# Units 12 to 23 of a chunked RWKV-5 attention beside a SwiGLU block: 64 steps of two batches a unit instead of 128 steps of one

## The chip, the cores and the metric

The kernel runs on one core of a Trainium2 chip. The core has a matrix engine (PE, with its weight loads shown apart as PEld), a vector engine (DVE), a scalar engine (ACT), GpSimd (POOL) and SyncE (SP), which here issues most of the DMAs. The metric is device microseconds of one execution, lower is better.

## The reference, cut to what matters

```python
# r, k, v: (4 batches, 8 heads, 768 steps, 48); w, u: (8, 48)
for t in range(S):
    cur = einsum('bhd,bhe->bhde', u[None] * kt, vt)
    y[:, :, t] = einsum('bhd,bhde->bhe', rt, state + cur)
    state = w[None, :, :, None] * state + einsum('bhd,bhe->bhde', kt, vt)
x = y.transpose(0, 2, 1, 3).reshape(B * S, H * D)          # (3072, 384)
g = x @ w_gate                                             # w_gate, w_val: (384, 1536)
out = (g / (1 + exp(-g)) * (x @ w_val)) @ w_out            # w_out: (1536, 384)
```

All of it is in float32.

## The kernel before, in words

**Units.** The 768 steps of each of the 4 batches are cut in 6 chunks of 128 steps. A unit i is chunk i // 4 of batch i % 4, so there are 24 units. In a unit the scores of a head are a 128x128 product of turned keys and turned r, masked below the diagonal. On the diagonal stands the sum of r, k and u (`own_sum`, DVE; `diagonal`, ACT: eight times the identity scaled by a column of `du`). The decay w is worked into k and r beforehand by tables (`scale_k`, `scale_r`, POOL), so that the state needs one factor a chunk.

**What a unit does on PE.** `scores(i)` (L459) writes two banks of PSUM, one for the even and one for the odd heads. `outputs(i)` (L512) makes the turned y, 384 rows by 128 steps, in 32-row tiles, four of them side by side in the array: for each tile one product of the state `Z` with turned r, and one or two of `v_ld` with the masked scores `At`. ACT copies the bank to `xT` (L516). `update(i)` (L527) makes the chunk's part of the new state, which DVE adds to `Z` (L539) and POOL multiplies by w to the 128th (L540). Units 20 to 23 need no update.

**From unit 12 on** the scores are computed in halves of 64 keys: 64x128 and 64x64 pieces, so that the quarter above the diagonal is not computed. So that the DMAs that turn k and r can stay inside such halves, the steps of the upper four heads stand swapped in the partitions (`places`, `in_order`, the second mask). k and r are not turned on PE from unit 10 on: `move_blocks` has SP move 32x32 blocks of `hats` within SBUF (L416, 16 DMAs a unit from unit 12 on), and `turn_blocks` has DVE transpose them in place (L437, twice a unit).

**Order.** Each engine's order is that of the recorded program. Step s of the loop (L1288) prepares unit s + 1 (`scale_k`, `scale_r`, `own_product` on POOL), computes `scores(s - 1)`, and from step 12 on `outputs(s - 2)` and `update(s - 2)` right behind it. The rest of PE's time is filled with the feed-forward work of finished units, which stands in `todo`: `gaps(s, n)` takes a share of it at five places in a step. This work is `gate_value` (L550), `project` (L625) and, from pair 2 on, `three_step` (L806), a product of 3x3 blocks in 15 rounds instead of 18. Its sums are evicted from four banks by DVE and ACT (L830), its gates are computed by ACT (L837), and its weight sums are made by POOL (L736). Each `feed` also takes one waiting diagonal (`small`) and one waiting masked copy (`lazy`). The attention's own banks are a ring of four (`next_psum`): a step takes two for scores, one for outputs, one for the update.

**SP's queue** holds, in order, the loads of k and r for unit s + 3 (6 DMAs), the moves for unit s + 1 (16) and the loads of v for unit s + 1 (6). On even steps the loads of k and r stand behind those of v, since `scale_r` comes late there.

Step 26 ends the loop's work; from there a tail of `three_units` and `project_thirds` runs to the end.

Of the kernel before, what the change touches and what calls it, by code (L numbers as in the profile page):

```python
# [15 lines left out]
P = 128  # L16
# [6 lines left out]
def fast(  # L23
# [47 lines left out]
    w128 = cst.tile([P, HP], FP32, name="w128")  # L71
    held = cst.tile([P, HP], FP32, name="held")
# [27 lines left out]
    Z = [cst.tile([P, HP, D2], FP32, name=f"Z{b}") for b in range(B)]  # L100
# [23 lines left out]
    SWAPPED = 12  # L124

    def places(i, n):

        if i < SWAPPED:
            return [(slice(0, P), slice(0, n), 0)]
        return [  # L130
            (slice(0, P), slice(0, n // 2), 0),
            (slice(0, 64), slice(n // 2, n), 64),
            (slice(64, P), slice(n // 2, n), -64),
        ]

    def load(i):
        c, b = divmod(i, B)
        for src, dst in zip((k, r), raw(i)):
            for p, h, o in places(i, H):
                rows = slice(P * c + p.start + o, P * c + p.stop + o)  # L140
                sp.dma_start(out=dst[p, h], in_=src[b, h, rows, :].rearrange("h t d -> t h d"))

    def load_v(i):
        c, b = divmod(i, B)
        for e in range(2):
            for p, a, o in places(i, HP):
                rows = slice(P * c + p.start + o, P * c + p.stop + o)
                sp.dma_start(
                    out=v_ld[i % 4][p, a, 64 * e : 64 * e + D],
                    in_=v[b, :, rows, :].rearrange("(a e) t d -> e t a d", e=2)[e][:, a],  # L150
                )
# [129 lines left out]
    for z in Z:  # L281
        pool.memset(z[:], 0.0)
# [14 lines left out]
    def warm(n, bank=None):  # L297
# [12 lines left out]
    pool.memset(mask[:], 1.0)  # L310
    pool.affine_select(
        out=mask[:], in_=mask[:], compare_op=ALU.is_gt, fill=0.0,
        base=0, pattern=[[0, 2], [1, P]], channel_multiplier=-1,
    )
    pool.memset(mask[0:64, 1, 64:P], 0.0)
    pool.memset(mask[64:P, 1, 0:64], 1.0)
# [24 lines left out]
    def at(i, a):  # L341

        return HP - 1 - a if i >= BLOCKS and i % 2 == (i < SWAPPED) else a

# [19 lines left out]
    def diagonal(i, on_act=None):  # L364

        du = dus.pop(i)
        on_act = on_act or (HP if i < 4 else H)
# [28 lines left out]
    def move_blocks(i):  # L396
# [4 lines left out]
        if i < SWAPPED:  # L401
# [10 lines left out]
        for m in range(4):  # L412
            for q in range(4):
                src = h[32 * q : 32 * q + 32, P * first + 32 * m : P * first + 32 * m + 1]
                dst = h[32 * m : 32 * m + 32, P * 31 + 32 * q : P * 31 + 32 * q + 1]
                sp.dma_start(  # L416
                    out=bass.AP(
                        tensor=dst.tensor, offset=dst.offset,
                        ap=[list(dst.ap[0]), [-P, 2 * HP], [1, 32]],
                    ),  # L420
                    in_=bass.AP(
                        tensor=src.tensor, offset=src.offset,
                        ap=[list(src.ap[0]), [P * step, 2 * HP], [1, 32]],
                    ),
                )

    def turn_blocks(i):
# [5 lines left out]
        for n, (dst, src) in enumerate(((kT[i % 2], blocks[0]), (turned[i], blocks[1]))):  # L433
            if i < SWAPPED:
# [8 lines left out]
    def scores(i):  # L443
# [4 lines left out]
        whole, left, right = slice(0, P), slice(0, 64), slice(64, P)  # L448
        if i < SWAPPED:
            parts = [(a, whole, whole) for a in range(HP)]  # L450
        else:
            parts = []
            for a in range(HP // 2):
                parts += [(a, left, whole), (a, right, right)]
                parts += [(a + HP // 2, right, whole), (a + HP // 2, left, left)]
        for a, keys, cols in parts:
            for e in range(2):
                rows = slice(64 * e, 64 * e + D)
                pe.matmul(  # L459
                    ps[e][keys, a, cols],  # L460
                    kT[i % 2][rows, at(i, a), keys], turned[i][rows, at(i, a), cols],
# [3 lines left out]
        def masked_copy(e):  # L465
            if i < SWAPPED:
                dst = At[i % 2][:].rearrange("p (a e) t -> p a e t", e=2)[:, :, e]
                m = mask[:, 0].bitcast(INT32).unsqueeze(1).to_broadcast([P, HP, P])
                dve.copy_predicated(dst, m, ps[e][:])
                return  # L470
            dst = At[i % 2][:].rearrange("p (o a e) t -> p o a e t", o=2, e=2)[:, :, :, e]
            m = mask[:].bitcast(INT32).unsqueeze(2).to_broadcast([P, 2, HP // 2, P])
            dve.copy_predicated(dst, m, ps[e][:].rearrange("p (o a) t -> p o a t", o=2))
# [6 lines left out]

    def outputs(i):

        c, b = divmod(i, B)
# [5 lines left out]
        def in_order(x, a):  # L491
            if i < SWAPPED or a < HP // 2:
                return x
            return bass.AP(
                tensor=x.tensor, offset=x.offset + 64,
                ap=[list(x.ap[0]), [-64, 2], [1, 64]],
            )

# [19 lines left out]
    def update(i):  # L518
        c, b = divmod(i, B)
        if c == NCH - 1:  # L520
            return
# [766 lines left out]
    for s in range(4, N + 2):  # L1288
        if 4 < s < N:
            own_sum(s)  # L1290
# [496 lines left out]
```

## Time and profile before

| what | us |
|---|---|
| median of 3 runs (590.78 to 591.75) | 591.72 |
| profiled execution, span from first to last instruction | 590.1 |
| median less that span | 1.6 |
| PE busy / PEld busy | 579.1 / 520.6 |
| DVE busy / POOL busy / ACT busy | 424.3 / 352.5 / 226.9 |
| scores of unit 12, the first that the change touches, start at | 156.9 |
| outputs of unit 23, the last, end at | 427.5 |
| granted PE clock, mean | 0.998 of full |

The span was taken in one profiled execution, which is not one of the three that were timed. What lies outside it, 1.6 us by the median, is the start and the end that show no instruction. A step that the change touches is therefore worth in the median what it is worth in the span. [...] Durations of PE records overlap, since matmuls are pipelined, so the time that a group takes is read from where the next group starts.

### The profile page before, as it was taken

To read this page: it belongs to the slowest core of one execution; us is meant where nothing else is said; L and a number is where in the kernel's file an instruction comes from. 1 tells how busy PE (TensorE), PEld (TensorE's weight loads), DVE (VectorE), ACT (ScalarE), POOL (GpSimd) and SP (SyncE) were. 2 spreads that over 40 slices of the span, in tenths; PEclk is the share of its full clock that TensorE was granted. 3 is DMA by queue.
4 is the path that set the end of the run, shared out by engine and by line. 5 is a ranking of instruction groups with operands and counts; after the bars stand their busy time and mean duration, and the time that the engine had idled before them with its cause. 6 is when DMAs were issued, how large, how long until landed. Compare 5 with 4: busy or idle time off the path is not lost.

```text
span 590.1 us, 13203 instructions
## 1 busy us (share of the span) xinstructions
PE 579.1 (98%) x5210; PEld 520.6 (88%) x5210; DVE 424.3 (72%) x713; ACT 226.9 (38%) x523; POOL 352.5 (60%) x375
## 2 busy tenths in 40 slices
PE   8889999999999999999999999999999999999996
PEld 7778888899888899988899988889988899988896
DVE  7878786489588877578887477879257878377682
ACT  4559786321443422244331344423134320233310
POOL 6689888989999402977600996513678970011610
PEclk9999999999999999999999999999999999999999
DMA  7999978641342323233234233200100000100001
GB/s 196 220 240 248 270 249 87 70 70 40 78 77 38 54 48 70 48 63 54 39 57 79 67 55 55 47 14 2 54 2 1 1 1 1 55 0 1 1 1 57
DMA packets 148004, 41.48 MB, mean 70 GB/s; under 512 B 138465, under 2 KB 141794, under 8 KB 147938
## 3 DMA queue, kind: packets, MB, share of 16 engines
q1 hardware_dynamic: 144770, 36.27, 30.7%
q10 hardware_dynamic: 3168, 4.33, 2.0%
q8 instruction: 42, 0.69, 0.5%
q14 instruction: 24, 0.20, 0.1%
HBM read 28.31 MB, written 4.72 MB: 56 GB/s over the span
## 4 chain that ended last, share of the span: by engine, by line
PE 95%; DVE 2%; DMA 1%; issue 0%; POOL 0%; ACT 0%; POOLq 0%; DVEq 0%
PE bank L806 32%; PE bank L625 18%; PE ring L806 13%; PE bank L550 11%; PE bank L1032 8%; PE ring L512 6%; PE ring L459 3%; PE ring L390 1%; PE ring L1032 1%; PE ring L527 1%; DMA hats<-in_r_dram 1%; PE ring L301 1%; DVE hv L830 0%; PE bank L354 0%; PE ring L305 0%
## 5 line engine op out<-in xcount | busy, mean ns | idle before, releaser
L830 DVE TENSOR_TENSOR hv<-hv,bank 128x512 f32<-128x512 f32 x132 | 87.2, 681 | 25.9 <-PE bank L806 14.0
L369 ACT ACTIVATE At<-ident,du 128x128 f32<-128x128 f32 x180 | 61.0, 398 | 14.1 <-DVE du L270 6.1
L550 PE MATMUL bank<-xT,wgv 128*128 128x256 f32 x288 | 66.2, 384 | 0.0
L806 PE MATMUL bank<-xf,wgv 128*128 128x256 f32 x256 | 65.9, 382 | 0.0
L830 ACT COPY hv<-bank 128x512 f32<-128x512 f32 x72 | 40.2, 586 | 57.1 <-PE bank L806 50.7
L550 PEld LDWEIGHTS bank<-xT,wgv 128*128 128x128 f32 x288 | 53.4, 190 | 8.0
L736 POOL TENSOR_TENSOR s<-wgv 128x256 f32<-128x256 f32 x39 | 29.8, 788 | 49.0 <-PE bank L625 48.9
L806 PEld LDWEIGHTS bank<-xf,wgv 128*128 128x128 f32 x256 | 47.8, 190 | 7.0 <-DVE kT L1077 0.6
L1086 POOL TENSOR_TENSOR hv<-At,hats 128x512 f32<-128x512 f32 x8 | 10.2, 1273 | 66.0 <-ACT At L1085 66.0
L540 POOL TENSOR_TENSOR Z<-Z,w 48x192 f32<-48x192 f32 x32 | 16.9, 528 | 36.7 <-DVE Z L539 35.5
L837 ACT ACTIVATE hv<-hv 128x512 f32<-128x512 f32 (+1 forms) x33 | 21.2, 667 | 45.4 <-DVE hv L830 45.2
L512 PE MATMUL ring<-At,v_ld 128*32 128x128 f32 x768 | 35.1, 273 | 2.1 <-ACT xT L516 1.4
L806 PE MATMUL bank<-xT,wgv 128*128 128x256 f32 x144 | 35.8, 381 | 0.0
L806 PE MATMUL bank<-xT,s 128*128 128x256 f32 x152 | 35.5, 381 | 0.0
L625 PE MATMUL bank<-wt,hs 128*128 128x192 f32 x192 | 33.7, 328 | 0.6 <-DVE hs L599 0.6
L625 PE MATMUL bank<-wo,hs 128*128 128x192 f32 x192 | 33.9, 327 | 0.0
L625 PE MATMUL bank<-wo,hv 128*128 128x192 f32 x192 | 33.4, 327 | 0.0
L512 PEld LDWEIGHTS ring<-At,v_ld 128*32 128x32 f32 x768 | 30.5, 110 | 3.3 <-ACT xT L516 1.6
L806 PEld LDWEIGHTS bank<-xT,s 128*128 128x128 f32 x152 | 28.5, 190 | 4.8 <-issue 0.8
L625 PEld LDWEIGHTS bank<-wt,hs 128*128 128x128 f32 x192 | 31.3, 190 | 1.4 <-ACT At L369 0.8
L625 PEld LDWEIGHTS bank<-wo,hv 128*128 128x128 f32 x192 | 31.6, 190 | 0.4
L625 PEld LDWEIGHTS bank<-wo,hs 128*128 128x128 f32 x192 | 31.6, 190 | 0.3
(227 smaller groups left out, 1398.9 us busy)
## 6 DMA issues: line engine op xcount, KB each, us to landing
hats<-hats SPq DMA_DIRECT2D x192, 32.0 KB, 2.0
w_bits<-in_moe_w_gate_dram SPq DMA_DIRECT2D x6, 768.0 KB, 6.1
w_bits<-in_moe_w_val_dram SPq DMA_DIRECT2D x6, 768.0 KB, 6.9
w_bits<-in_moe_w_out_dram SPq DMA_DIRECT2D x6, 768.0 KB, 6.9
out_dram<-hv ACTq DMA_DIRECT2D x22, 192.0 KB, 1.9
v_ld<-in_v_dram SPq DMA_DIRECT2D x24, 96.0 KB, 5.8
k_ld<-in_k_dram SPq DMA_DIRECT2D x8, 192.0 KB, 3.5
r_ld<-in_r_dram SPq DMA_DIRECT2D x8, 192.0 KB, 4.0
```

The source lines that it names most:

```text
L369: lambda h=h: act.activation(At[i % 2][:, h, :], ident[:], AF.Identity, scale=du[:, h : h + 1])
L459: pe.matmul(ps[e][keys, a, cols], kT[i % 2][rows, at(i, a), keys], turned[i][rows, at(i, a), cols], start=True, stop=True, skip_group_chec ...
L512: pe.matmul(ps[32 * q : 32 * q + 32, cc, :], *x, start=start, stop=stop, skip_group_check=True,)
L540: pool.tensor_mul(ze, ze, w)
L550: pe.matmul(gv[:, o, :].rearrange("p (i t) -> p i t", i=2), wt[:, c, P * f : P * (f + 1)], xT[:, 2 * g % NX : 2 * g % NX + 2, c, :], start ...
L625: pe.matmul(ps, lhs[:, f, :], rhs[:, f, :], start=(f == 0 and n in (0, 1, 4)), stop=(f == FH - 1), skip_group_check=True,)
L736: op(made[o], made[a], made[b])
L806: pe.matmul(ps[:, o], u[:, o], v, start=first and o == 0, stop=True, skip_group_check=True,)
L830: do(out, *(pair_of(wide[a][:]) if isinstance(a, str) else a for a in args))
L837: todo.append((at, lambda: act.activation(gate, gate, AF.Silu)))
L1032: pe.matmul(ps, (h[what][q] if h[what] is D_ else h[what][:, q])[:, f, :], wide["o"][what][:, f, :], start=first and f == 0 and (split or ...
L1086: todo.append((muls, lambda: on.tensor_mul(h, sg, value)))
```

## The change

From unit 12 on a unit is 64 steps of two batches: partitions 0 to 63 hold one batch, 64 to 127 the other (`part`, `pieces_of`). There are still 24 units. The units 12 to 23 are now 6 chunks of 64 steps for each pair of batches, so the state of a batch is needed again after two units, not after four.

- **Outputs.** For batch p one tile of `At` (`both(i)[:, p]`) holds the masked 64x64 scores on one half of the partitions and turned r on the other half. `v_ld` of the batch holds v on the first half and the state on the other. One product over all partitions then gives both parts of y. A unit's outputs are 32 matmuls of 64 columns; before they were 28 of 128 columns.
- **Scores** are 16 matmuls of 64 keys by 64 columns in four 64x64 tiles of the array; before, 8 had 128 columns and 8 had 64.
- **Update** is 16 matmuls of 64x48 (before 32x48) into two banks of the ring (before one), for units 12 to 21 (before 12 to 19). DVE adds in four pieces instead of two, POOL multiplies two tiles of 48x384 instead of two of 48x192, by w to the 64th (`w64`). The state stays in `v_ld`; units 8 to 11 put theirs there by two DMAs each.
- **Diagonal**: eight scaled 64x64 identities a unit go to `own`, which lies over the old `Z`. `fill(i)` is new: four DMAs of SP, two for turned r and two for `own`, into `At`, where the masked copies then write the scores (four of 64x256, before two of 128x512).
- **Order.** `outputs(s - 2)` stands ahead of `scores(s - 1)` from step 14 on, `update(s - 2)` behind it. `diagonal(s)` is taken at the start of step s and flushed before `fill(s)` at the step's end. `load_v(s)` follows `update(s - 2)`.
- **DMAs of SP for a unit**: 4 loads of k and r (6), 4 of v (6), 8 moves (16), 4 fills (none). Results of units 12 to 23 are stored in two DMAs of 64 rows instead of one of 128.
- The helpers of the swapped order go, and the tables' lower halves are copied over the upper ones once.

PE's order in step 14: `rT` and `kT` are turned r and k, `Z` is the state before, `ring` are the attention's banks, `bank` those of the feed-forward work; rows that repeat are left out. Before:

```order
L459 MATMUL ring3_98<-rT_1881,kT1_115 64x128
L459 MATMUL ring0_95<-rT_1881,kT1_115 64x128
L459 MATMUL ring3_98<-rT_1881,kT1_115 64x64
L459 MATMUL ring0_95<-rT_1881,kT1_115 64x64
L512 MATMUL ring1_96<-rT_1657,Z0_99 32x128 x4
L512 MATMUL ring1_96<-At0_112,v_ld0_107 32x128 [waits DMAHW1_49]
L527 MATMUL ring2_97<-v_ld0_107,hats_111 32x48 x16
L806 MATMUL bank2_93<-xT_88,wgv_86 128x256 [waits DVE_49]
```

Now, at the same place (L550 is the new outputs, L516 the new scores, L567 the new update, L922 the old L806):

```order
L550 MATMUL ring3_99<-At0_110,v_ld0_105 32x64 [waits DMAHW6_49,DMAHW7_49,DMAHW2_49,DMAHW0_49]
L550 MATMUL ring3_99<-At0_110,v_ld0_105 32x64
L550 MATMUL ring3_99<-At0_110,v_ld1_106 32x64 [waits DMAHW4_49,DMAHW1_49,DMAHW0_49]
L516 MATMUL ring0_96<-rT_1873,kT1_113 64x64 x2
L516 MATMUL ring1_97<-rT_1873,kT1_113 64x64 x2
L567 MATMUL ring2_98<-v_ld0_105,hats_109 64x48 x2
L567 MATMUL ring3_99<-v_ld1_106,hats_109 64x48 [waits Activation_49]
L922 MATMUL bank2_94<-xT_89,wgv_87 128x256 [waits DVE_49]
```

The outputs moved ahead of the scores, and the second bank of the update is ring3, the bank that the outputs of the same step have just filled: the update waits for ACT's copy of it.

SP's order for the steps 16 and 17, from the moves for unit 17 on (`zs` holds `own`). Before:

```order
L416 DMA hats<-hats 32x8x32 x16
L148 DMA v_ld_108<-in_v_dram 128x2x48
L148 DMA v_ld_108<-in_v_dram 64x2x48 x2
L148 DMA v_ld_108<-in_v_dram 128x2x48
L141 DMA k_ld_106<-in_k_dram 128x4x48
L141 DMA k_ld_106<-in_k_dram 64x4x48 x2
```

Now:

```order
L435 DMA hats<-hats 32x16x32 x8
L147 DMA k_ld_104<-in_k_dram 64x8x48 x2
L147 DMA r_ld_102<-in_r_dram 64x8x48 x2
L503 DMA At_110<-rT 64x512
L504 DMA At_110<-zs 64x512
L153 DMA v_ld_107<-in_v_dram 64x4x48 x2
L153 DMA v_ld_108<-in_v_dram 64x4x48 x2
```

The loads of v no longer follow the moves; the four fills (two rows of each kind) stand at the end of a step's DMAs, behind the eight moves for the next unit.

The core of the diff:

```diff
+    zs = cst.tile([P, B, HP * D2], FP32, name="zs")
+    own = zs[:].rearrange("p b x -> p (b x)")[:, 0 : 2 * H * 64].rearrange(
...
+    def part(i, p):
+        c, q = divmod(i - PAIRED, 2)
+        return 2 * q + p, PAIRED // B * P + 64 * c
...
-        for m in range(4):
-            for q in range(4):
-                src = h[32 * q : 32 * q + 32, P * first + 32 * m : P * first + 32 * m + 1]
...
+        for p in range(2):
+            for n in range(2):
+                for m in range(2):
+                    q, o = 64 * p + 32 * n, 64 * first + 32 * m
+                    src = h[q : q + 32, o : o + 1]
...
+    def fill(i):
+        rT = turned[i][:].rearrange("p a (e t) -> p (a e) t", e=2)
+        for p in range(2):
+            there, here = slice(64 - 64 * p, P - 64 * p), slice(64 * p, 64 * p + 64)
+            sp.dma_start(out=both(i)[there, p], in_=rT[there])
+            sp.dma_start(out=both(i)[here, p], in_=own[here, i % 2])
+
+    def paired_scores(i, ps):
...
+        for n in range(HP):
+            for p in range(2):
+                rows = slice(64 - 64 * p, 64 - 64 * p + D)
+                for g in range(2):
+                    o = 64 * (p ^ g)
+                    pe.matmul(
+                        ps[p][o : o + 64, n, :], kt[rows, n + HP * g, :], rT[rows, n + HP * g, :],
...
+        def masked_copy(p, g):
+            rows, o = slice(64 * p, 64 * p + 64), 64 * (p ^ g)
+            m = mask64[rows].bitcast(INT32).unsqueeze(1).to_broadcast([64, HP, 64])
+            dve.copy_predicated(both(i)[rows, p, HP * g : HP * g + HP], m, ps[p][o : o + 64])
...
+        lazy.popleft()()
+        lazy.popleft()()
+
+    def paired_outputs(i):
+        ps = next_psum(CC, P)
...
+                vz, x = v_ld[part(i, p)[0]], both(i)[rows, p]
...
+                pe.matmul(
+                    ps[32 * q : 32 * q + 32, cc, 64 * p : 64 * p + 64], *x,
...
+        act.copy(xT[:, i % NX, :, :], ps[:])
+
+    def paired_update(i):
+        if i + 2 >= N:
+            return
+        ps = [next_psum(HP, D) for _ in range(2)]
...
+                    pe.matmul(
+                        ps[p][o : o + 64, n, :], khat[i % 4][rows, h, :],
+                        v_ld[part(i, p)[0]][rows, a, 64 * e : 64 * e + D],
...
+            ze = state(slice(0, HP))
+            pool.tensor_mul(ze, ze, w64[o : o + D].unsqueeze(3).to_broadcast([D, HP, 2, D]))
...
     for s in range(4, N + 2):
+        if PAIRED <= s < N:
+            diagonal(s)
...
         gaps(s, 0)
+        if s > N:
+            outputs(s - 2)
         if 4 <= s - 1 < N:
-            while small:
-                small.popleft()()
+            if s <= PAIRED:
+                flush()
+            if s - 2 >= PAIRED:
+                outputs(s - 2)
             scores(s - 1)
+            if LATE <= s < PAIRED + 2:
+                outputs(s - 2)
             if s >= LATE:
-                outputs(s - 2)
                 update(s - 2)
+            if PAIRED <= s < N:
+                load_v(s)
             gaps(s, 1)
...
-        if s < N:
+        if s < PAIRED:
             diagonal(s)
+        elif s < N:
+            flush()
+            fill(s)
```

More of the change, by code (lines that the diff above doesn't have):

```diff
@@ L366, in diagonal @@
         du = dus.pop(i)
+        if i >= PAIRED:
+            small.extend(
+                lambda h=h: act.activation(
+                    own[:, i % 2, slot(i, h), :], ident64, AF.Identity, scale=du[:, h : h + 1]
+                )
+                for h in range(H)
+            )
+            return
         on_act = on_act or (HP if i < 4 else H)
```

233 lines of the change are left out of this document (143 added, 90 removed).

## The prediction

> **What bounds the kernel now.** I read the page first: its busy times and the chain that ended last.
>
> ```profile
> span 590.1 us, 13203 instructions
> PE 579.1 (98%) x5210; PEld 520.6 (88%) x5210; DVE 424.3 (72%) x713; ACT 226.9 (38%) x523; POOL 352.5 (60%) x375
> PE 95%; DVE 2%; DMA 1%; issue 0%; POOL 0%; ACT 0%; POOLq 0%; DVEq 0%
> ```
>
> PE is the bound: busy for 98% of the span and 95% of the chain. The next question is whether PE waits for anything in the stretch of the change. The windows answer for two steps (after the stretch: its length, the busy time of PE, PEld, DVE, ACT and POOL, the granted clock, the DMA share, GB/s), and the waits from 150 to 430 us for all of them (total, times, longest).
>
> ```profile
> 160.00:180.00 20.00, 20.00 (x199) 17.31 (x199) 16.59 (x27) 7.71 (x19) 19.14 (x26) 1.00 0.39 65
> 180.00:200.00 20.00, 20.00 (x93) 16.92 (x92) 17.19 (x25) 9.31 (x19) 18.67 (x22) 1.00 0.27 42
> ```
>
> ```profile
> PEld bank L806 <- ACT hv L830: 1.9, 6, 0.4
> PEld bank L625 <- ACT At L369: 0.8, 1, 0.8
> PE bank L625 <- DVE hs L599: 0.6, 1, 0.6
> ```
>
> PE has no gap at a clock of 1.00, and the three largest sums of its waits for other engines are 3.3 us in eight places, none above 0.8. So every PE nanosecond removed here is worth its full length, if nothing new holds PE up. But DVE is busy 83 and 86% of these windows: it has 2.8 to 3.4 us to spare in 20. Last I read PE's timeline of step 14 and the durations of L527's records.
>
> ```profile
> 175.64 0.90 PE L459 MATMUL ring<-rT,kT 48*64 48x128 f32 x32
> 176.47 0.43 PE L512 MATMUL ring<-rT,Z 112*32 112x128 f32 x8
> ...
> 177.81 0.40 PE L512 MATMUL ring<-At,v_ld 128*32 128x128 f32 x8
> 178.03 0.52 PE L527 MATMUL ring<-v_ld,hats 128*32 128x48 f32 x32
> 178.48 1.99 PE L806 MATMUL bank<-xT,wgv 128*128 128x256 f32 x8
> L527 PE MATMUL ring<-v_ld,hats x640: 204/206/231, 27.1 to 348.1; 128*32 128x48 f32 x160
> ```
>
> One step's attention takes PE 2.84 us: scores 0.83, outputs 1.56, update 0.45. These 34 us in 12 steps are all that the change can shorten.
>
> **The change part by part.** *The price of a column.* Each product stands as two records, and four tiles run side by side. The update's 32 records take 0.52 us less the 0.206 of the last one: 31 intervals of 10.1 ns, 40.5 ns for four at 48 columns, 0.84 ns a column. The outputs' 56 records take 1.56 us: 14 fours of 111 ns at 128 columns, 0.87 ns a column. Columns set the pace in both, so 64 columns cost 54 to 56 ns for a group of four.
>
> *Outputs*: 32 products of 64 columns are 64 records, 16 fours of 56 ns, 0.90 us. They also wait for more semaphores (some six more waits of PE's queue a unit, which I put at 0.1 us). 1.56 - 1.00 = 0.56 us a unit, times 12: **-6.7 us** (-6.2 to -7.5).
>
> *Scores*: 32 records as before, but of 64 columns where the mean was 96: eight fours lose 32 columns each, 8 x 32 x 0.84 = 0.21 us a unit: **-2.4 us** (-1.5 to -3).
>
> *Update*: units 20 and 21 get one that they did not have, 2 x 0.45 = 0.9. The weight tile is 64 wide instead of 32 while the columns stay 48, so a four costs between 40.5 ns, as now, and 57, as four 64-wide tiles at 64 columns: +0 to 1.3 over ten units. **+1.3 us**, nearer the lower end since columns set the pace in the rows above.
>
> *The update's second bank* is the bank that this step's outputs have just filled, so PE now waits there for ACT's copy of y. Behind that matmul the whole feed-forward stream is queued. ACT's timeline gives the copy, and what ACT does when the attention starts at the three places where it is late:
>
> ```profile
> 178.28 0.48 ACT L516 COPY xT<-ring 128x384 f32<-128x384 f32 x1 [2.60 <-PE ring L512]
> ```
>
> ```profile
> 278.47 0.79 PE L459 MATMUL ring<-rT,kT 48*64 48x128 f32 x26
> 302.76 0.79 PE L459 MATMUL ring<-rT,kT 48*64 48x128 f32 x26
> 386.16 0.90 PE L459 MATMUL ring<-rT,kT 48*64 48x128 f32 x32
> ```
>
> ```profile
> 278.58 1.07 ACT L830 COPY hv<-bank 128x512 f32<-128x512 f32 x2 [0.28 <-PE bank L806]
> 304.79 0.84 ACT L837 ACTIVATE hv<-hv 128x768 f32<-128x768 f32 x1 [3.03 <-DVE hv L830]
> 305.54 0.97 ACT L369 ACTIVATE At<-ident,du 128x128 f32<-128x128 f32 x3
> 387.40 1.07 ACT L830 COPY hv<-bank 128x512 f32<-128x512 f32 x2 [1.41 <-DVE hv L830]
> ```
>
> Let T be the start of a step's attention. PE would come to the second bank at T + 1.7 (outputs 1.0, scores 0.55, first half of the update 0.2). ACT's copy can begin 0.25 us after the last output matmul starts (178.28 less 178.03) and takes 0.48: T + 1.0 + 0.25 + 0.48 is 1.73, and with the lead at a change of shape some 1.85. With ACT free the wait is thus 0 to 0.2; 0.15 in seven of the ten steps, 1.05. In the others ACT is late. Step 18: its two evictions end at 279.65, T + 1.18; a diagonal (about 0.3, a third of the 0.97) and the copy (0.48) follow, T + 1.96, a wait of 0.26. Step 19: the gate ends at 305.63, T + 2.87; T + 3.65, a wait of 1.95. Step 23: 388.47, T + 2.31; T + 3.09, a wait of 1.39. Together **+4.6 us**. Bounds: +1, if the shortened stream moves ACT's late work elsewhere; +6, if two more steps become like step 23.
>
> The Trainium skill, "TensorEngine Tiling (Array Packing)", PSUM Bottleneck, speaks against the change: tiling speeds up TensorE, not the evacuation of PSUM, and the copy may become the bottleneck. Here the copy keeps its 0.48 us while the outputs lose a third; by that page the wait stays, and the trace's ACT rows agree.
>
> *DVE* copies a unit's masked scores in four pieces instead of two, and adds the state in four instead of two.
>
> ```profile
> L473 DVE COPY_PREDICATED At<-mask,ring 128x512 f32<-128x512 int32 x24 | 17.8, 740 | 10.3 <-ACT At L369 8.0 <-PE ring L459 2.2
> 178.69 0.74 DVE L539 TENSOR_TENSOR Z<-ring,Z 48x192 f32<-48x192 f32 x2 [1.24 <-PE ring L527]
> 179.65 0.69 DVE L830 TENSOR_TENSOR hv<-hv,bank 128x512 f32<-128x512 f32 x1 [0.21 <-PE bank L806]
> ```
>
> A mask of half the columns I take at 0.40 (half of 0.74 and a little; bounds 0.37 and 0.74): 4 x 0.40 less 2 x 0.74 is +0.1 us. The adds keep their shape, 0.37 each: +0.74. DVE comes back to the evictions some 0.8 us later a step. In the row above it then waited 0.21 for PE, so it has little in hand, and the banks of L806, which are four, run out a few us later. In the five steps whose feed-forward work is L806 (14, 17, 18, 21, 22) I put 0.2 us each on PE; the least is 0, the most the whole 0.8. +1.0 (0 to 4).
>
> *The fills* are new on SP, behind the moves for the next unit, and these wait for DVE's turning. Step 17, the shortest, from SP's timeline, with the landing times (KB each, median us):
>
> ```profile
> 264.90 2.06 SPq L141 DMA_DIRECT2D k_ld<-in_k_dram  x3
> ...
> 271.89 11.22 SPq L416 DMA_DIRECT2D hats<-hats  x16
> ```
>
> ```profile
> hats<-hats SPq DMA_DIRECT2D x192, 32.0 KB, 2.0
> out_dram<-hv ACTq DMA_DIRECT2D x22, 192.0 KB, 1.9
> hats<-hats SPq DMA_DIRECT2D x8, 128.0 KB, 5.5
> swapped<-scales SPq DMA_DIRECT2D x2, 96.0 KB, 4.6
> ```
>
> An issue takes SP 0.70 us (11.22 / 16). Moves and loads become fewer (28 to 16 a unit, with four fills 20). From 271.89, eight moves and two fills end at 278.7 to 278.9; they land 2.0 to 2.5 later, about 281. The masked copy of that unit wants its tile at 278.47 + 1.6, about 280.1: 1 us late, and DVE stands behind it. The other steps are longer by up to 9 us, except 20. I put +0.5 on PE (0 to 1); at 4.6 us to landing it is a rival.
>
> *POOL* multiplies twice the state, 2 x 0.5 us more a unit, long after which it is needed (two steps later): 0. *The end*: results go out in two DMAs instead of one, one ACT issue more in the tail: **+0.4** (0 to 0.7).
>
> Sum: -6.7 - 2.4 + 1.3 + 4.6 + 1.0 + 0.5 + 0.4 = -1.3. The profiled execution becomes 588.8; the median of the runs shown is 1.6 above its span, so 590.4.
>
> **The rivals.** *The columns' gain is kept.* ACT's late work in steps 19 and 23 is feed-forward work whose place against the attention is not fixed: PE's steps get shorter, so the same gate may fall ahead of T or well behind the copy. Then the wait is the 1.05 of an idle ACT, and DVE uses the slack of its 2.8 us in 20: -6.7 - 2.4 + 1.3 + 1.05 + 0.4 = -6.3, 585.4. For it: the largest wait of PE or its weight loads is now 0.8. Against it: the copies keep their order on ACT's queue.
>
> *Slower: the fills land late.* The fill writes 64 rows of 2 KB, 128 KB, and the two rows of such size within SBUF show 5.5 and 4.6, not 2.0. At 4.6 the tile of step 17 comes 3.2 us late instead of 1, that of step 20 some 2.5, that of 21 some 1; DVE's queue stands, its evictions behind it, and PE's four banks fill after 0.9 us each. Of 6.7 us PE would lose some 4 above the 1.5 counted: 590.4 + 4 = 594.4. It decides from a landing of about 3 us. For it: the two rows. Against it: the 2.0 and 1.9 of single DMAs; the longer rows may have had others in flight.
>
> *Slower: a small matmul has a floor.* If a record could start no sooner than 25 ns after the one before, 64 records of outputs would take 1.6 us (+0.04 a unit instead of -0.56), and the scores 0.8 (no gain): 590.4 + 7.2 + 2.4 = 600. The update's records, 10.1 ns apart, speak against it. The Trainium skill, "TensorE: Matmul & The Clock Gate", section "Wait — 56ns, not 53.3ns?", gives this floor of about 25 ns whatever the columns. By that page it would be 600; the trace's 10.1 ns disagrees, and only if 64x64 tiles ran less side by side than 32-wide ones would it come back.
>
> **How the numbers follow.** Most of the gain eaten by the waits, 590.4: 0.55, own range 587.5 to 592.9 (ACT's wait 1.7 to 6, DVE's and fills' 0 to 4, not all at one end). The gain kept, 585.4: 0.22. Late fills, 594.4: 0.18. The floor, 600: 0.05. The range 584.5 to 595.0 takes in the first three but for their far ends. A measurement of this kernel tells 0.2%, 1.2 us, from no change. So faster (under 590.5): 0.29 of the 0.55, which has its middle at the bound, and the 0.22, 0.51. Same (to 592.9): 0.21 of the 0.55 and a little of the fills, 0.22. Slower: 0.27, of it 0.05 from the first case.
>
> **What would show it.** In the new profile, PE from the first L550 row to the first L516 row should be 0.9 to 1.0 us, the scores 0.5 to 0.6. The waits should name PE for ACT's L554, longest in steps 19 and 23, 3.5 to 5 us in all. Waits of L946 banks for DVE should stay below 2. The fills should land in under 3 us; if DVE's masked copy waits for a DMA by over 2 us a time, the slower rival holds. If PE has no wait for ACT above 0.8, the forecast is too high by 4. If the outputs take 1.5 us, the floor holds.

## The result and the profile after

The changed kernel takes 599.23 us (median of 4 runs, 598.31 to 600.5), the kernel before beside it 591.44: ratio 1.0136, 95% interval 1.0117 to 1.0156. It is 7.8 us slower; the forecast was 590.4, the range 584.5 to 595.0. The profiled execution, one of the shorter of the four, has a span of 596.6 us, 6.5 above that of before.

The page of the changed kernel, its span, its busy times and its chain:

```profile
span 596.6 us, 13553 instructions
PE 575.0 (96%) x5370; PEld 514.7 (86%) x5370; DVE 440.7 (74%) x761; ACT 223.4 (37%) x529; POOL 361.0 (61%) x382
PE 75%; DVE 10%; POOL 5%; DMA 3%; issue 2%; ACT 2%; ACTq 1%; SPq 1%; DVEq 0%; POOLq 0%
```

PE has 4.1 us less to do than before (579.1), as was meant, but the span is longer: PE stands still for 21.6 us instead of 11.0. The chain says the same: it ran over PE for 95%, now for 75%. DVE has 16.4 us more to do.

PE's timeline of step 14, the step that the prediction showed:

```profile
174.31 1.11 PE L550 MATMUL ring<-At,v_ld 112*32 112x64 f32 x64
175.35 0.69 PE L516 MATMUL ring<-rT,kT 48*64 48x64 f32 x32
175.88 0.81 PE L567 MATMUL ring<-v_ld,hats 64*64 64x48 f32 x32
176.61 2.00 PE L922 MATMUL bank<-xT,wgv 128*128 128x256 f32 x8
```

From row to row: outputs 1.04 us (before 1.56), scores 0.53 (0.83), update 0.73 (0.45). So PE's own part of the step went from 2.84 to 2.30 us. What was lost lies outside these rows. Five of the waits from 150 to 440 us (total, times, longest):

```profile
DVE At L524 <- PE ring L516: 10.4, 9, 2.9
PEld bank L922 <- ACT hv L946: 5.2, 6, 2.2
DVE At L524 <- DMA At<-zs: 4.6, 2, 3.0
PEld bank L922 <- DVE hv L946: 3.5, 5, 2.0
PEld ring L567 <- ACT xT L554: 3.1, 2, 1.8
```

Before, PE's weight loads for L806 waited 1.9 us for ACT. Now PE waits for ACT's and DVE's evictions and, in the update, for ACT's copy of y. The longest stalls as PE's timeline has them, with the idle time and what ended it in brackets:

```profile
186.47 1.75 PE L922 MATMUL bank<-xT,s 128*128 128x256 f32 x7 [0.79 <-DVE hv L946]
217.13 2.22 PE L738 MATMUL bank<-wt,hs 128*128 128x192 f32 x12 [1.02 <-DVE hs L712]
276.16 1.13 PE L922 MATMUL bank<-xf,s 128*128 128x256 f32 x4 [1.76 <-ACT hv L946]
308.00 0.67 PE L567 MATMUL ring<-v_ld,hats 64*64 64x48 f32 x28 [1.69 <-ACT xT L554]
355.49 1.13 PE L922 MATMUL bank<-xf,wgv 128*128 128x256 f32 x4 [1.59 <-DVE hv L946]
394.12 0.67 PE L567 MATMUL ring<-v_ld,hats 64*64 64x48 f32 x28 [1.14 <-ACT xT L554]
517.30 1.13 PE L922 MATMUL bank<-xT,s 128*128 128x256 f32 x4 [0.87 <-ACT kT L1196]
```

By the starts of PE's matmuls against their running pace (from 0.25 us up), the feed-forward work from 150 to 400 us stands still 8.75 us in nine places, the updates 3.25, and 1.4 us are lost at 432 and 517 us. Of these, the kernel before had none (one stall of 0.7 us behind 400 us stands in both). Of the nine, six end with an eviction of DVE, 5.3 us, and three with one of ACT, 3.4.

### The profile page after: what moved, and what is told of

Read it like the earlier page. It is cut to its first block, busy times and chain, and to the rows that moved or that the text cites. A ratio compares the mean times of both kernels' runs of the same rounds, so it can differ in the third digit from the quotient of the medians.

```text
span 596.6 us, 13553 instructions
## 1 busy us (share of the span) xinstructions
PE 575.0 (96%) x5370; PEld 514.7 (86%) x5370; DVE 440.7 (74%) x761; ACT 223.4 (37%) x529; POOL 361.0 (61%) x382
## 4 chain that ended last, share of the span: by engine, by line
PE 75%; DVE 10%; POOL 5%; DMA 3%; issue 2%; ACT 2%; ACTq 1%; SPq 1%; DVEq 0%; POOLq 0%
PE bank L922 22%; PE bank L738 12%; PE ring L922 12%; PE bank L663 10%; PE bank L1151 8%; DVE hv L946 4%; PE ring L617 2%; PE ring L550 2%; POOL wgv L825 2%; POOL s L852 2%; DMA v_ld<-in_v_dram 2%; PE ring L473 1%; PE ring L405 1%; PE ring L1151 1%; DVE At L524 1%
## 5 line engine op out<-in xcount | busy, mean ns | idle before, releaser
L922 PE MATMUL bank<-xf,wgv 128*128 128x256 f32 x256 | 66.3, 383 | 1.9 <-DVE hv L946 1.9
L922 PEld LDWEIGHTS bank<-xf,wgv 128*128 128x128 f32 x256 | 47.7, 190 | 9.7 <-DVE hv L946 3.1
L589 POOL TENSOR_TENSOR v_ld<-v_ld,w 48x384 f32<-48x384 f32 x20 | 16.5, 825 | 45.5 <-DVE v_ld L585 27.7
L922 PE MATMUL bank<-xT,s 128*128 128x256 f32 x152 | 36.0, 382 | 2.1 <-DVE hv L946 1.1
L922 PE MATMUL bank<-xT,wgv 128*128 128x256 f32 x144 | 35.9, 382 | 0.0
L922 PEld LDWEIGHTS bank<-xT,s 128*128 128x128 f32 x152 | 28.5, 190 | 7.6 <-issue 2.0
L524 DVE COPY_PREDICATED At<-mask,ring 64x256 f32<-64x256 int32 x48 | 21.3, 443 | 15.9 <-PE ring L516 10.4
L376 ACT ACTIVATE zs<-mask,du 128x64 f32<-128x64 f32 x96 | 29.0, 343 | 9.1 <-DVE hv L751 4.1
L852 POOL TENSOR_TENSOR s<-s 128x256 f32<-128x256 f32 x39 | 30.6, 784 | 0.9
```

Of the source, the lines that this page charges most:

```text
L376: lambda h=h: act.activation(own[:, i % 2, slot(i, h), :], ident64, AF.Identity, scale=du[:, h : h + 1])
L524: dve.copy_predicated(both(i)[rows, p, HP * g : HP * g + HP], m, ps[p][o : o + 64])
L589: pool.tensor_mul(ze, ze, w64[o : o + D].unsqueeze(3).to_broadcast([D, HP, 2, D]))
L852: op(made[o], made[a], made[b])
L922: pe.matmul(ps[:, o], u[:, o], v, start=first and o == 0, stop=True, skip_group_check=True,)
```

## The experiments

All were timed in five rounds beside the kernel before on the same chip. Differences in us are differences of the ratios times 590.7; those against the changed kernel, which was timed at another time, carry both intervals, 1.2 us each way for the changed kernel and 0.5 to 1.1 for the run (a_up_late 2.0).

| run | ratio to before, 95% interval | median us |
|---|---|---|
| changed kernel | 1.0136 (1.0117 to 1.0156) | 599.23 |
| b_dve | 1.0017 (1.0008 to 1.0027) | 591.63 |
| b_order | 1.0014 (1.0002 to 1.0027) | 591.54 |
| b_dve3 | 1.0178 (1.0159 to 1.0197) | 600.36 |
| b_lazy | 0.9999 (0.9990 to 1.0008) | 590.66 |
| a_half_adds | 1.0083 (1.0065 to 1.0102) | 595.71 |
| a_up_late | 1.0480 (1.0447 to 1.0514) | 618.58 |
| a_up_late2 | 1.0097 (1.0082 to 1.0112) | 596.02 |
| a_spread | 1.0167 (1.0149 to 1.0185) | 600.13 |
| a_fill | 1.0117 (1.0103 to 1.0132) | 597.22 |
| a_store1 | 1.0383 (1.0365 to 1.0401) | 613.56 |
| a_lazy | 1.0095 (1.0082 to 1.0108) | 596.08 |
| a_all | 1.0038 (1.0026 to 1.0051) | 592.78 |
| a_all_scores | 1.0058 (1.0045 to 1.0071) | 593.80 |
| a_all_sp | 1.0046 (1.0031 to 1.0062) | 592.84 |
| a_all_half | 0.9960 (0.9947 to 0.9973) | 588.36 |
| a_best | 1.0008 (0.9998 to 1.0018) | 591.51 |
| a_best_nomul | 1.0000 (0.9991 to 1.0008) | 590.85 |
| a_best_lazy | 0.9930 (0.9917 to 0.9944) | 586.80 |

The theories at the start were D (DVE's added work makes the evictions late, and PE waits for these) and A (DVE has time to spare, ACT's and SP's queues make the waits). A grew into Q, which gives each new queue order its price. The letters L, B and P are explained in the expectations that use them.

**b_dve and b_order: DVE's work alone, PE's order alone, on the kernel before.**

```diff
 # b_dve
-            lazy.append(lambda e=e: masked_copy(e))
+            for o in range(1 if i < SWAPPED else 2):
+                lazy.append(lambda e=e, o=o: masked_copy(e, o))
...
                 dve.tensor_add(ze, ps[rows], ze)
+                if i >= SWAPPED:
+                    dve.tensor_add(ps[rows], ps[rows], ze)
 # b_order
+            if s >= LATE + 2:
+                outputs(s - 2)
             scores(s - 1)
-            if s >= LATE:
+            if LATE <= s < LATE + 2:
                 outputs(s - 2)
```

> The kernel before with nothing but more DVE work of the kind that the change brings: from unit 12 on each masked copy is cut in two pieces of 128x256, and each of the two state adds of units 12 to 19 is followed by one more add of 48x192 whose result, in the bank, nobody reads. Theory D (DVE is the second bound; its time before the evictions is what PE waits for): some 9 us of DVE work more in the stretch, of which PE loses 3 to 6: 594.5 to 597.5 us, with new waits of the L806 banks for DVE. Rival A (DVE's slack takes its extra work, the new waits come from ACT's and SP's queues alone): within 1 us of before.

> The kernel before with nothing but the new order of PE: from step 14 on the outputs stand ahead of the scores. Theory D: DVE's first masked copy stands at the head of its queue and now waits some 1.5 us longer for the scores, with the evictions behind it: +1 to +2.5 us, 592.5 to 594. Rival A: PE's work is the same, no change within 0.7 us.

Measured: +1.0 and +0.8 us. Neither alone does what D expected; the two together were not run. In b_dve's waits from 150 to 430 us, PE waits for DVE's evictions into `hv` thus, and for the one in L604 1.2 us in two waits (before, 0.6 in one):

```profile
PEld bank L811 <- DVE hv L835: 0.6, 2, 0.3
```

The kernel before bears four adds in a row, and cut copies, for 1.0 us. D in its simple form falls.

**a_half_adds: two of four adds left out of the changed kernel.**

```diff
-            for g in range(2):
+            for g in range(1):
                 x = 64 * (1 - (p ^ g))
```

> The changed kernel with two of the four state adds of a unit left out (half of the heads' state is not brought up to date): DVE does 0.71 us less in each of ten steps, all else stays. Theory D: PE's waits for DVE's evictions in steps 14 to 22 shrink: 3 to 5 us less than the changed kernel, about 595. Rival A: within 1 us of the changed kernel, 598.2 to 600.2.

Measured: 3.1 us less than the changed kernel. So there two adds fewer a unit are worth three times what two adds more, with the cut copies, cost in b_dve, and A falls as well.

**a_up_late and a_up_late2: the update behind the second share of feed-forward work.**

```diff
-            if s >= LATE:
+            if LATE <= s < PAIRED + 2:
                 update(s - 2)
 # a_up_late: load_v(s) stays here; a_up_late2: it follows the update
             gaps(s, 1)
+            if s >= PAIRED + 2:
+                update(s - 2)
```

> The changed kernel with the update put behind the second share of feed-forward work instead of ahead of it, so that ACT's copy of y is done before PE reaches the update's second bank. Both theories expect the waits of the update in steps 19 and 23 (3.25 us) to go. Rival A: 3.3 us less than the changed kernel, 596. Theory D: half of it comes back as waits for DVE's evictions, since PE reaches its banks sooner: 1 to 2.5 us less, 597 to 598.

> The changed kernel with the update behind the second share of feed-forward work, and the loads of v behind the update, since they write over the v that it reads. The waits of the update for ACT's copy in steps 19 and 23 (3.25 us) should go. Theory Q (each new queue order holds PE up by itself: update 3.25, diagonals on ACT 2.7, late fill 2.5, stores 1.4 us): 3 us less than the changed kernel, about 596. Theory D (DVE's time is what PE waits for in the end): half of it comes back, 597 to 598.

a_up_late lost 20 us: the loads of v now stood ahead of the update, which so read the v of a later unit and waited 15.8 us for its DMAs. It says nothing on ACT. a_up_late2, with the loads behind the update: 2.3 us less than the changed kernel (3.2 by the medians). Its PE timeline of step 19:

```profile
305.78 2.22 PE L738 MATMUL bank<-wo,hv 128*128 128x192 f32 x12
307.92 0.68 PE L567 MATMUL ring<-v_ld,hats 64*64 64x48 f32 x32
```

The update runs in one piece, without the 1.69 us. The stall went, and most of its time with it; little came back as waits for DVE. By the time alone Q's 3 us and D's 1 to 2.5 are not told apart.

**a_spread and a_fill: diagonals two at a time; fills ahead of the moves.** The changed kernel takes one diagonal with each piece of feed-forward work and the rest in one go ahead of the fills. In step 17 its ACT timeline has:

```profile
274.12 1.53 ACT L376 ACTIVATE zs<-mask,du 128x64 f32<-128x64 f32 x6
275.55 1.04 ACT L946 COPY hv<-bank 128x512 f32<-128x512 f32 x2
```

Six diagonals stand ahead of an eviction, and PE at 276.16 waits for just this eviction. SP's timeline ahead of step 21 shows why the fills come late:

```profile
339.35 5.40 SPq L435 DMA_DIRECT2D hats<-hats  x8
344.80 1.33 SPq L147 DMA_DIRECT2D k_ld<-in_k_dram  x2
346.18 1.31 SPq L147 DMA_DIRECT2D r_ld<-in_r_dram  x2
347.53 1.66 SPq L503 DMA_DIRECT2D At<-rT  x1
349.29 0.54 SPq L504 DMA_DIRECT2D At<-zs  x1
```

And DVE's, where 3.03 us go by ahead of the masked copies, with the adds, the turning and the evictions behind them:

```profile
351.71 0.90 DVE L524 COPY_PREDICATED At<-mask,ring 64x256 f32<-64x256 int32 x2 [3.03 <-DMA At<-zs]
352.62 1.48 DVE L585 TENSOR_TENSOR v_ld<-ring,v_ld 48x192 f32<-48x192 f32 x4
354.02 0.70 DVE L456 STREAM_TRANSPOSE kT<-hats 128x512 f32<-128x512 f32 x1
354.75 1.88 DVE L946 TENSOR_TENSOR hv<-hv,bank 128x512 f32<-128x512 f32 x3
```

```diff
 # a_spread, in gaps
-            feed(share[0] // 5 + ... )
+            feed(share[0] // 5 + ... , 2 if s >= PAIRED else 1)
 # a_fill: also
+        if PAIRED <= s < N:
+            flush()
+            fill(s)
         if BLOCKS <= s + 1 < N:
             move_blocks(s + 1)
...
-        elif s < N:
-            flush()
-            fill(s)
```

> The changed kernel with two diagonals taken with each piece of feed-forward work instead of one, so that none are left to be flushed in one go at the end of a short step (in step 17 six of them, 1.5 us of ACT, stand ahead of an eviction). Theory Q: 1.9 us less than the changed kernel, 597.3. Theory D: under 0.7 us less, since ACT's eviction is late there because DVE is.

> As the run with two diagonals at a time, and the fills put ahead of the moves for the next unit on SP, right behind DVE's turning: they land some 5 us earlier. Theory Q: the waits of DVE for the fill (4.6 us) go and with them PE's 2.5 us in step 21: 4.4 us less than the changed kernel, 594.8. Theory D: 1 us less at most. A third case: the moves, now 2.6 us later, hold up the next turning, and nothing is won.

a_spread: 1.8 us more than the changed kernel (the intervals touch), a miss for both theories. It hardly took the row of diagonals apart: in step 17 ACT still runs five of them (1.29 us) ahead of the eviction, and PE waits 1.53 us for it. And two diagonals instead of one now stand ahead of ACT's copy of y, so that the update of step 19 waits longer (1.92 against 1.69), and those of steps 18 and 23 by as much:

```profile
307.77 0.67 PE L567 MATMUL ring<-v_ld,hats 64*64 64x48 f32 x28 [1.92 <-ACT xT L554]
```

a_fill, with the same spreading: 1.1 us less than the changed kernel (the intervals touch; Q had said 4.4, D 1 at most), 3.0 less than a_spread. SP issues the fills of that unit 11.6 us earlier, and DVE no longer waits for them:

```profile
335.89 0.52 SPq L503 DMA_DIRECT2D At<-rT  x1
```

But the edit moves two things, since the flush of the diagonals goes ahead of the moves together with the fills. PE's wait behind the diagonals in step 17, in a_spread and then in a_fill:

```profile
275.51 1.13 PE L922 MATMUL bank<-xf,s 128*128 128x256 f32 x4 [1.53 <-ACT hv L946]
```

```profile
274.17 1.13 PE L922 MATMUL bank<-xf,s 128*128 128x256 f32 x4 [0.34 <-ACT hv L946]
```

In step 21 PE's waits went from 1.64 and 0.57 us to one of 1.09. So the 3.0 us are not of the fills alone, and no run moved the flush without them.

**a_store1: one store for both halves.**

```diff
-                for rows, b, t in pieces_of(...): act.dma_start(out=out[n0 : n0 + 64, :], in_=...)
+                act.dma_start(out=bass.AP(..., ap=[[S * DM, 2], [DM, 64], [1, DM]]), in_=...)
```

> The changed kernel with one DMA for both halves of a unit's result (a pattern of two batches by 64 rows by 384) instead of two: ACT issues 12 fewer. Theory Q: PE's wait for ACT at 517 us (1.04) and part of what the tail lost go: 1 to 1.4 us less, about 598. Theory D: no change.

Measured: 14.6 us more. ACT's timelines at 510 to 520 us, here and in the changed kernel: two such stores hold ACT for 4.78 us, where four of the plain ones took 3.21.

```profile
516.06 4.78 ACTq L147 DMA_DIRECT2D out_dram<-hv  x2
```

```profile
510.82 3.21 ACTq L1116 DMA_DIRECT2D out_dram<-hv  x4
```

Most of the loss lies at the very end: from PE's last matmul to the end of the span it is 16.4 us (595.6 to 612.0), in the changed kernel 5.3 (591.3 to 596.6). Why this pattern is so slow stays open. It tells nothing on the two stores.

**a_all, a_all_scores, a_all_sp, a_all_half: the edits together.** a_all is a_up_late2 with a_fill. a_all_scores puts `scores(s - 1)` ahead of `outputs(s - 2)` again, a_all_sp also gives the second store to SP, a_all_half also leaves out two adds.

```diff
 # a_all_sp
-                act.dma_start(
+                (sp if rows.start else act).dma_start(
```

> The changed kernel with the update behind the second share, two diagonals at a time and the fills ahead of the moves. Theory Q: the single gains of 3.2 and 2.0 us add up, and the waits that the diagonals alone brought to the update (0.45 and twice 0.23) are gone with the update's own: 593 to 594. Theory D: the gains do not add, PE then waits for DVE instead: 595 to 596.

> As the run before, with the scores ahead of the outputs again. DVE's masked copies wait 10 us for the scores in the changed kernel; with the scores first they start 1 us earlier a step. Theory D: 1 to 2 us less than the run before. Theory Q: no change within 0.7, since PE does the same work and nothing is queued differently for it.

> As the run before, with the second of the two stores of a unit issued by SP instead of ACT. Theory Q: ACT's six issues in a row at 511 to 517 us (0.65 each) become three, and PE's wait for ACT there (0.7 to 1.6) goes: 1 us less than the run before. Rival: the wait at 516 is not of the stores, no change.

> As the run before, with two of the four state adds of a unit left out (half of the heads' state is not brought up to date). What DVE's extra adds still cost when the other queues are mended. Theory D: 2 to 4 us less than the run before. Theory Q: within 1 us of it.

a_all: 5.8 us less than the changed kernel, more than its parts (2.3 and 1.1): with the update out of ACT's way the spreading does no harm. The update's waits for ACT's copy, 2.8 us on PE in the changed kernel and 3.5 in a_fill, are gone. a_all_scores: 1.2 us more, a miss for both. With the scores first, the update's second bank is one that the scores have filled, so PE waits for DVE's masked copy, here in step 17:

```profile
266.31 0.67 PE L567 MATMUL ring<-v_ld,hats 64*64 64x48 f32 x28 [0.50 <-DVE At L524]
```

DVE's 10 us of waiting for the scores were thus little loss of PE's: they fell from 10.3 in a_all to 3.7 here, and nothing was won. a_all_sp: 0.7 us less than a_all_scores (1.0 by the medians), and no gap at 512 us in PE's timeline; the wait at 517 was the stores':

```profile
510.30 1.89 PE L922 MATMUL ring<-xf,s 128*128 128x256 f32 x8
512.02 1.03 PE L922 MATMUL bank<-xT,s 128*128 128x256 f32 x4
```

a_all_half: 5.1 us less than a_all_sp, above D's 2 to 4. So with the other queues mended, DVE's adds are the largest loss left, while b_dve had shown two more adds a unit, with the cut copies, to cost 1.0 on the kernel before.

**b_dve3, a_best, a_best_lazy, a_best_nomul: work, burst or POOL.** b_dve3 cuts the copies as b_dve does and puts three unread adds behind each add of the kernel before. a_best is a_all with the second store by SP. a_best_lazy takes its adds one at a time; a_best_nomul leaves POOL's multiplication out.

```diff
 # a_best_lazy
-                dve.tensor_add(ze, ps[p][x : x + D]..., ze)
+                lazy.append(lambda add=add, g=g: add(g=g))
```

> The kernel before with the masked copies cut in two and three (not one) unread adds behind each state add of units 12 to 19: some 18 us of DVE work more instead of 7.2. Theory D with slack (DVE has about 7 us in the stretch that nobody waits for; what goes beyond is paid by PE): 594 to 598. Theory L (each us of DVE costs PE the same 0.14 us as the 7.2 us did): 593.

> The changed kernel with all that won time: update behind the second share, two diagonals at a time, fills ahead of the moves, second store by SP; outputs ahead of the scores as in the change. Theory Q and D alike: 592.8 less 1.0 for the stores, 591.8, still no faster than before.

> As the run before, with the four state adds of a unit taken one at a time with the next pieces of feed-forward work instead of in a row. DVE's total is the same. Theory D with burst (1.5 us of adds in a row make the evictions behind them late): 2 to 3 us less than the run before, 589 to 590. Theory D with total (DVE's time in the stretch is short as a whole): no change within 0.7.

> As the run with all that won time, with POOL's multiplication of the state left out (the decay of the state is not applied). DVE's own work is the same. Theory P (DVE's operations on SBUF alone stretch from 0.7 to 1.8 us while POOL works, and POOL's longer multiplications push its other work under them): 1.5 to 3 us less. Theory D: within 0.7 us of the run with all that won time.

b_dve3: +10.5 us, above both ranges. a_best: +0.5, not told from the kernel before. a_best_lazy: 4.6 us less than a_best, more than the 2 to 3 expected, and the one version with all of its work that beats both kernels. a_best_nomul: 0.5 less than a_best, not clear of the noise and within what D allowed; POOL's multiplication is not what a_best loses by. The busy lines of b_dve3 and of a_best_lazy, each with the wait of PE's weight loads for DVE's evictions into `hv` from 150 us to 440:

```profile
PE 581.7 (97%) x5210; PEld 520.2 (87%) x5210; DVE 442.8 (74%) x785; ACT 227.6 (38%) x523; POOL 352.5 (59%) x375
PEld bank L812 <- DVE hv L836: 6.2, 6, 1.7
```

```profile
PE 575.3 (98%) x5370; PEld 515.1 (88%) x5370; DVE 441.9 (75%) x761; ACT 223.7 (38%) x529; POOL 369.0 (63%) x382
PEld bank L926 <- DVE hv L950: 0.5, 1, 0.5
```

DVE is busy the same 442 us in both; in the one PE waits 6.2 us for it, in the other 0.5. a_best, which differs from a_best_lazy by the spreading alone, has DVE busy for 435.7 us, 6 less, and is 4.6 us slower. So it is not the total of DVE's work that PE pays here, but how much stands in a row ahead of an eviction.

**a_lazy and b_lazy: the spreading alone.** The same edit on the changed kernel, and on the kernel before for its two adds.

> The changed kernel with one edit alone: the four state adds of a unit are taken one at a time with the next pieces of feed-forward work, not in a row. The update stays where the change put it, with its wait for ACT's copy. Theory B (burst: 1.5 us of adds in a row make the evictions behind them late): 3 to 5 us less than the changed kernel, 594 to 596. If the spreading only won because the other queues were mended first: under 1.5 us less.

> The kernel before with the same edit: its two state adds of units 12 to 19 are taken one at a time with the next pieces of feed-forward work. Theory B: PE waits for DVE hardly anywhere there, so within 0.7 us of before: the spreading pays only what the change lost. Rival: the spreading is a gain of its own, 2 us or more less than before, and the changed kernel with it owes its lead to that alone.

a_lazy: 2.4 us less than the changed kernel (3.2 by the medians), between the two expectations of 3 to 5 and under 1.5. b_lazy: no change. So the spreading is no gain of its own; it gives back what the change's adds in a row had cost. DVE's timeline of step 14 in the changed kernel, and in a_lazy:

```profile
176.08 0.89 DVE L524 COPY_PREDICATED At<-mask,ring 64x256 f32<-64x256 int32 x2 [0.67 <-PE ring L516]
176.98 1.48 DVE L585 TENSOR_TENSOR v_ld<-ring,v_ld 48x192 f32<-48x192 f32 x4
178.50 0.69 DVE L946 TENSOR_TENSOR hv<-hv,bank 128x512 f32<-128x512 f32 x1
```

```profile
175.78 0.89 DVE L524 COPY_PREDICATED At<-mask,ring 64x256 f32<-64x256 int32 x2 [0.98 <-PE ring L516]
177.48 0.69 DVE L950 TENSOR_TENSOR hv<-hv,bank 128x512 f32<-128x512 f32 x1 [0.81 <-PE bank L926]
183.25 0.36 DVE L585 TENSOR_TENSOR v_ld<-ring,v_ld 48x192 f32<-48x192 f32 x1
```

In the changed kernel DVE's first eviction starts at once behind the adds, 1.9 us after PE took up the feed-forward work (176.61); in a_lazy DVE is back early and waits 0.81 us for PE.

a_lazy also shows that the causes act together. The fills stand at the same place of SP's queue as in the changed kernel, and in step 21 DVE still waits 1.96 us for them. But no adds follow in a row, and PE runs on without a gap, where the changed kernel stood for 1.59 and 0.57 us. DVE's and then PE's timeline of step 21 in a_lazy:

```profile
349.40 0.90 DVE L524 COPY_PREDICATED At<-mask,ring 64x256 f32<-64x256 int32 x2 [1.96 <-DMA At<-zs]
```

```profile
353.37 2.00 PE L926 MATMUL bank<-xf,s 128*128 128x256 f32 x8
```

## Why the prediction was wrong, step by step

- **Outputs, right.** Forecast 1.00 us a unit and -6.7 in all; measured 1.04 and -6.6 (eight of 1.57 and four of 1.68 before, eleven of 1.04 and one of 1.27 now).
- **Scores, too low.** Forecast -2.4, where its own 0.21 us a unit gives -2.5; measured -3.4, beyond its bound of -3: the lead at the change of kind went too (0.83 to 0.53 us a step).
- **Update, mis-sized.** Forecast +1.3 with "nearer the lower end since columns set the pace"; measured +3.75 (ten of 0.73 without the waits, against eight of 0.45). A group of four with 64-wide weight tiles takes 58 ns by the starts of its records, at 48 columns as at 64, the upper bound that the forecast had named; the first two groups of an update take 137 and 94.
- **The update's wait for ACT, right in mechanism and place.** Forecast 4.6 with 1.95 in step 19 and 1.39 in step 23; by the starts 1.82 and 1.28, with 0.15 in step 18, 3.25 in all. The 1.05 us that it had put on the seven steps with an idle ACT did not come. With the update moved, in a_up_late2, these waits are gone.
- **Terms so far:** -6.6 - 3.4 + 3.75 + 3.25 = -3.0, where the forecast had -3.2. Up to here its sum stood, but by luck: the scores came out 1.0 us better, the update 2.4 worse, the wait 1.3 better, and these cancel.
- **DVE's evictions and the fills: the step that failed.** The forecast put "+1.0 (0 to 4)" and "+0.5 on PE (0 to 1)", 1.5 us together; PE's stalls in the feed-forward work are 8.75 us. Three causes show, and they act together. The first is DVE's adds in a row, which the forecast took as a delay of 0.8 us a step with a price of 0.2: spreading them gave back 2.4 us by a_lazy, 4.6 by a_best_lazy. The second is the fills: DVE waited 3.03 us in step 21, where the forecast took the fill of step 17, 1 us late, for the worst. They landed about as fast as it took, by the issues:

```profile
At<-rT SPq DMA_DIRECT2D x24, 128.0 KB, 2.7
At<-zs SPq DMA_DIRECT2D x24, 128.0 KB, 2.5
```

  What it had left out is that on even steps four loads of k and r (2.6 us) stand between the moves and the fills; the first fill's issue also took 1.66 us there, against 0.52 in a_fill. That makes the rival of late fills right in its consequence and wrong in its cause, and it takes more than the late fill to stop PE in step 21: in a_lazy DVE waits 1.96 us for it, no adds follow in a row, and PE runs on. The third cause it did not name at all: the flush of diagonals on ACT, with PE's wait of 1.76 us in step 17. No run changed the flush alone.
- **The slack was read from shares.** The forecast reckoned of DVE that "it has 2.8 to 3.4 us to spare in 20". a_best against a_best_lazy shows that such a number does not decide. DVE's and PE's timelines of step 14 give the time from PE's first feed-forward matmul behind the attention to DVE's first eviction: 1.17 us before, 1.74 in b_dve (+1.0 us in all), 3.35 in b_dve3 (+10.5). On the kernel before the price rises far faster than this delay. It does not carry from one kernel to the other: the changed kernel has 1.89 there and loses 7.8 us, a_lazy 1.17 and loses 5.6.
- **The stores, mis-sized.** +0.4 forecast; 1.04 us of PE's wait at 517 us, which a_all_sp takes away.
- **The other rivals.** "The columns' gain is kept" fell with PE's waits for ACT. "A small matmul has a floor" gave 600, next to the measured time, by a mechanism that is not there: it wanted 1.6 us for the outputs, they took 1.04. A time that fits proves no cause. By the rule of the Trainium skill that stood beside it ("TensorE: Matmul & The Clock Gate", section "Wait — 56ns, not 53.3ns?", about 25 ns from start to start at least) 64 records could not have run in 1.04 us; they are 14 ns apart ((1.11 - 0.22) / 63).
- **The rule of the PSUM copy** in the Trainium skill ("TensorEngine Tiling (Array Packing)", PSUM Bottleneck), that the copy may become the bottleneck, told more than the forecast took from it. What empties PSUM held PE up here on both engines, ACT's copy by 3.25 us and DVE's adds by 2.4 to 4.6.

The sum by the trace, -3.0 + 8.75 + 1.4, is +7.15 for a span that grew by 6.5; some 0.2 of it, at 432 us, stands in the last outputs' 1.27 as well. Left open: why two adds a unit, with the cut copies, cost 1.0 us on the kernel before and two adds 3.1 to 5.1 on the changed one, when DVE's delay in step 14 is 1.89 us, little above b_dve's 1.74. There are ten such units instead of eight, which is too few to explain it. That PE's steps are shorter, so that DVE has less time to make up, fits, but no run took this alone.

## What to carry to other kernels

When a change shortens the bound engine, list what every other engine now does in a row between two of its evictions, not its busy share. Taking the same work one piece at a time between evictions gave 2.4 us on the changed kernel as it was and 4.6 us once its other queues were mended; only all these edits together turned a kernel that lost 1.4% into one that wins 0.7%. When a DMA is added to a queue, count all that stands ahead of it in each kind of step.

## What the runs showed of the hardware

DVE's product of two SBUF tiles stretched where POOL was already at work. In a_half_adds, DVE's and POOL's timelines at 182 us:

```profile
182.47 2.53 DVE L946 TENSOR_TENSOR hv<-hv 128x512 f32<-128x512 f32 x1
```

```profile
181.50 1.73 POOL L589 TENSOR_TENSOR v_ld<-v_ld,w 48x384 f32<-48x384 f32 x2
183.19 1.26 POOL L946 TENSOR_TENSOR hv<-hv 128x512 f32<-128x512 f32 x1
```

DVE's product ends 0.55 us after POOL's does (185.00 against 184.45), as if it had waited for that end. In the changed kernel it takes 1.82 us and ends 0.55 us after POOL's again (185.13 against 184.58). In a_lazy, where POOL's multiplications of the state are elsewhere, POOL's product ends 0.13 us after DVE's starts, and the same instruction takes 0.68 us (182.56 to 183.24, with POOL's end at 182.69). The Trainium skill, "SBUF — State Buffer", section "SBUF: two separate sides", says that DVE with two SBUF inputs and POOL share a port pair that one holds for a whole instruction; these three ends agree. What POOL's multiplication of the state adds to this weighs little in the whole kernel: a_best_nomul won 0.5 us, not clear of the noise.

By the starts of its records, a group of four tiles with 64-wide weights takes 58 ns whether 48 columns run through (L567) or 64 (L516), while 32-wide tiles took 40.5 ns at 48 columns (L527 before). And ACT pays 0.8 us for each of the four stores at 511 us that it issues in a row, so that splitting a store shows up as PE's wait for ACT's eviction at 517 us, which is not there in a_all_sp.
